# One more block's output by seven half products, its operand sums put on GpSimd and VectorE, and an earlier start of the second stage

## The chip, the cores and the metric

The kernel runs on one core of a Trainium2 chip. The metric is the time of one execution on the device in microseconds (us). A kernel is run several times in turn with the kernel before on the same chip. Each kernel is judged by the runs of the kernel before that were made beside it on its chip.

The engines are named as the profile names them: PE is TensorE (matmuls), PEld its weight loads, DVE is VectorE, ACT is ScalarE, POOL is GpSimd. SBUF and PSUM are two memories of the core: the kernel's operands lie in SBUF, TensorE's products go to PSUM, and a bank is a part of PSUM. A tag such as L386 is a line of the kernel. The lines of the changed kernel mostly lie one further down than those of the kernel before (L385 there is L386 here).

## The reference

```python
scores = (q_c @ k_c.T) / 8          # batch 8, heads 8, seq 576, dim 64, chunks of 64
attn = softmax(scores)              # inside each chunk of 64
x = (attn @ v_c)                    # laid out as 4608 tokens x 512
a = x @ w_a                         # 512 -> 1536
b = x @ w_b
out = (a * b) @ w_out               # 1536 -> 512, float32
```

## The kernel before

The attention works on units of 256 tokens (18 units), the feed-forward part on blocks of 512 tokens (9 blocks). TensorE is the engine that everything else is meant to keep busy.

- Block 0 computes its two projections plainly, in 12 steps of 512 columns (`ab_step`, ft 0 to 11). The attention of unit 2 is woven into its last steps.
- Block 1 computes them in 24 half steps of 256 columns, since unit 3 comes later than unit 2. It starts when `xT` of unit 2 is there.
- Blocks 2 to 8 use six groups each of seven half-size products in place of eight (a Strassen-like scheme). The price is sums of the operands, made beforehand: `combine_x` makes s1 to s4 of the tokens, `combine_w` makes t1 to t4 of the weights.
- The output of a block is made during the next block, in pieces between the products. Blocks 2 and on use seven half products for that too (`OutGroup`, 14 pieces). Their sums are `combine_ab` (of a\*b, tiles `so` and `ab_sb`) and `combine_wo` (of w_out, tiles `wot` and `wo`). The outputs of blocks 0 and 1 are plain.

The parts that the change and the argument touch, with cuts marked:

```python
def cast(U, names="qkv"):                       # float32 -> bfloat16
    for n in names if U < NU else "":
        raw[n, U] = raw_pool.tile([128, 2, H, D], BF16, name=f"{n}_raw")
        eng = nc.vector if U == 0 and n != "v" else nc.gpsimd
        eng.tensor_copy(out=raw[n, U], in_=staged.pop((n, U)))

def transpose_pe(U, names="qk"):
    # ...
        tp = bank().bitcast(BF16).rearrange("c (i m p) -> c i m p", i=2, m=NKT)   # ONE PSUM bank
        for i in range(2):
            # ... four transposes into tp[:, i] ...
        for i in range(2):
            cp = nc.vector.tensor_copy if w == 0 or U == 1 else nc.scalar.copy
            cp(out=dst[:, i], in_=tp[:, i].rearrange("c m (g p) -> c m g p", g=2))

def combine_wo(part, j):                         # sums of w_out, 128x512 f16, both operands in SBUF
    # ...
    o, x0, x1, op = (
        (t3, b22, b12, SUB), (t2, t3, b11, ADD), (t4, b21, t2, SUB), (t1, b12, b11, SUB)
    )[part]                                      # t1 lies in the place of b12
    nc.gpsimd.tensor_tensor(out=o, in0=x0, in1=x1, op=op)

def combine_ab(K, part, j, eng=None):            # sums of a*b, 128x512 f16, both operands in SBUF
    # ...
    o, x0, x1, op = (
        (s1, a21, a22, ADD), (s2, s1, a11, SUB), (a21, a11, a21, SUB), (s4, a12, s2, SUB)
    )[part]
    (eng or nc.gpsimd).tensor_tensor(out=o, in0=x0, in1=x1, op=op)

class Group:                                     # seven products of one group; each is 4 matmuls
    # p1, p6, p2, p5, p7, p3, p4; ScalarE copies results to u_sb, v_sb, b_sb
    def add7(self):                              # VectorE; p4 adds into pc after it
        self.c = c_pool.tile([128, 512], FP32, name="c_sb")
        nc.vector.tensor_tensor(out=self.c, in0=self.C, in1=self.v, op=ADD)
        nc.vector.tensor_tensor(out=self.C, in0=self.C, in1=self.u, op=ADD)
```

```python
# block 0, with the attention of unit 2
for ft in range(NFT):
    ab_step(0, ft)
    # ...
    if ft == 6:
        transpose_pe(2)
    if ft == 8:
        slot(2)                 # scores
    if ft == 10:
        slot(None, 2)           # sums, inverse (Ln and Exp on ScalarE), values -> xT of unit 2

# blocks 2 to 8; the order here is each engine's order of issue
for K in range(2, NBLK):
    for i in range(NWP):
        if i == 1:
            # K == 2: the plain output pieces of block 1 become available here
            # K > 2:  combine_ab(K - 1, 3, j) for j in 0..2, on GpSimd
        # ... bring(unit): loads and casts of the next unit; combine_wo pieces in block 2 ...
        now = Group(K, i)
        now.p1()
        if last:
            last.add7()
        chunk(...)              # output pieces
        if last:
            last.p3()
        # ...
        now.p6()
        if last:
            last.p4()
            finish(last)
        now.p2()
        chunk(...)
        now.p5()
        now.p7()
        last = now
```

The softmax here doesn't subtract the row's maximum and nothing guards it: scores larger than these inputs give would overflow.

## Time and profile before

The kernel before takes 310.87 us (median of 3 runs, 310.45 to 311.45). Its profiled execution has a span of 309.1 us.

| | before |
|---|---|
| TensorE busy | 293.2 of 309.1 us (95%) |
| mean granted TensorE clock | 1.00 |
| first matmul of the projections | 18.87 us |
| first half product of block 1 | 43.43 us, after a gap of 1.47 us |
| groups 0 and 1 of block 2 together | 9.14 us |

Below is the first table of the page of the kernel before: the busy time, its share of the span and the number of instructions for each engine.

```profile
PE 293.2 (95%) x3476; PEld 228.9 (74%) x3478; DVE 205.2 (66%) x342; ACT 194.0 (63%) x350; POOL 178.6 (58%) x168
```

This is the timeline of VectorE before: start, duration, engine, line, operation, output and inputs, shape, count, and in brackets the idle time before it with what ended it.

```profile
80.95 0.43 DVE L385 TENSOR_TENSOR s<-xT 128x512 f16<-128x512 f16 x1
...
82.09 1.26 DVE L385 TENSOR_TENSOR s<-xT,s 128x512 f16<-128x512 f16 x1
83.27 0.41 DVE L364 SCALAR_TENSOR_TENSOR ab_sb<-po,c_sb 128x256 f16<-128x256 f32 x1
83.60 2.33 DVE L129 TENSOR_TENSOR wa<-wa,wb 128x512 f16<-128x512 f16 x2
87.67 0.69 DVE L443 TENSOR_TENSOR c_sb<-pc,v_sb 128x512 f32<-128x512 f32 x1 [1.74 <-ACT v_sb L416]
```

The first and the second line are the same operation of the same shape: 0.43 us and 1.26 us. GpSimd is idle from 80.40 to 81.81, while the first runs; a cast of its own from 81.81 to 83.07 lies beside the second. The two sums `wa<-wa,wb` (2.33 us for both) run beside it too. The last line is `add7` of the first group.

The gap in front of block 1 shows in the timelines of TensorE and ScalarE. The first line is the first half product of block 1. The second is the Exp of unit 2's `inverse`, on which its `xT` depends.

```profile
43.43 0.60 PE L355 MATMUL pa<-xT,wb 128*128 128x256 f16 x4 [1.47 <-DVE xT L305]
...
41.00 1.06 ACT L282 ACTIVATE ln<-ln 128x1024 f32<-128x1024 f32 x1
```

### The profile page before, as it was taken

To read this page: it belongs to the slowest core of one execution; us is meant where nothing else is said; L and a number is where in the kernel's file an instruction comes from. 1 tells how busy PE (TensorE), PEld (TensorE's weight loads), DVE (VectorE), ACT (ScalarE), POOL (GpSimd) and SP (SyncE) were. 2 spreads that over 40 slices of the span, in tenths; PEclk is the share of its full clock that TensorE was granted. 3 is DMA by queue.
4 is the path that set the end of the run, shared out by engine and by line. 5 is a ranking of instruction groups with operands and counts; after the bars stand their busy time and mean duration, and the time that the engine had idled before them with its cause. 6 is when DMAs were issued, how large, how long until landed. Compare 5 with 4: busy or idle time off the path is not lost.

```text
span 309.1 us, 8485 instructions
## 1 busy us (share of the span) xinstructions
PE 293.2 (95%) x3476; PEld 228.9 (74%) x3478; DVE 205.2 (66%) x342; ACT 194.0 (63%) x350; POOL 178.6 (58%) x168
## 2 busy tenths in 40 slices
PE   2879989999999999999999999999999999999995
PEld 1534557866566768888888888888888888888884
DVE  3345663967866686567757776677668766965872
ACT  1643557448575657766877686768775867566531
POOL 0575656644538688936782777377737711780560
PEclk9999999999999999999999999999999999999999
DMA  7999999999989994698439943993493000300025
GB/s 233 303 382 279 274 326 344 246 228 200 272 209 221 222 240 120 91 251 220 125 70 244 241 130 86 215 293 94 102 174 134 6 0 2 136 3 3 0 77 197
DMA packets 138887, 54.03 MB, mean 175 GB/s; under 512 B 114016, under 2 KB 132960, under 8 KB 138848
## 3 DMA queue, kind: packets, MB, share of 16 engines
q1 hardware_dynamic: 138704, 53.36, 70.8%
q8 instruction: 27, 0.44, 0.6%
q10 hardware_dynamic: 144, 0.13, 0.1%
q14 instruction: 12, 0.10, 0.1%
HBM read 37.75 MB, written 9.44 MB: 153 GB/s over the span
## 4 chain that ended last, share of the span: by engine, by line
PE 81%; DVE 6%; ACT 4%; POOL 4%; issue 2%; DMA 2%; SPq 0%; DVEq 0%; POOLq 0%; ACTq 0%
PE pb L405 17%; PE pc L405 11%; PE pa L405 10%; PE po L541 9%; PE pq L541 8%; PE pb L609 3%; PE pb L355 3%; PE pc L355 3%; PE po L355 3%; DMA st<-in_q_dram 2%; PE pq L355 2%; POOL so L485 2%; PE pa L355 2%; PE pt L296 1%; PE pt L263 1%
## 5 line engine op out<-in xcount | busy, mean ns | idle before, releaser
L405 PEld LDWEIGHTS <-t 128*128 128x128 f16 x504 | 48.3, 98 | 9.9 <-issue 3.9
L443 DVE TENSOR_TENSOR c_sb<-pc,v_sb 128x512 f32<-128x512 f32 x42 | 28.8, 686 | 35.7 <-ACT v_sb L416 35.0
L485 POOL TENSOR_TENSOR so<-ab_sb 128x512 f16<-128x512 f16 x20 | 23.1, 1152 | 50.9 <-DVE ab_sb L455 50.9
L405 PE MATMUL pb<-s,wa 128*128 128x256 f16 x336 | 50.6, 273 | 0.1
L405 PE MATMUL pa<-xT,wb 128*128 128x256 f16 x336 | 50.4, 273 | 0.0
L416 ACT COPY u_sb<-pb 128x512 f32<-128x512 f32 x42 | 24.7, 587 | 24.8 <-PE pb L405 23.5
L541 PEld LDWEIGHTS <-ab_sb 128*128 128x128 f16 x336 | 32.9, 98 | 4.2 <-issue 0.4
L405 PEld LDWEIGHTS <-wb 128*128 128x128 f16 x336 | 32.9, 98 | 4.0
L405 PEld LDWEIGHTS <-wa 128*128 128x128 f16 x336 | 31.0, 98 | 6.2 <-issue 0.2
L203 POOL CAST k_raw<-st 128x1024 bf16<-128x1024 f32 x17 | 18.1, 1062 | 28.8 <-DMA st<-in_k_dram 28.8
L455 DVE SCALAR_TENSOR_TENSOR ab_sb<-pc,c_sb 128x512 f16<-128x512 f32 x42 | 28.9, 688 | 6.9 <-PE pc L405 5.5
L455 DVE SCALAR_TENSOR_TENSOR ab_sb<-pb,b_sb 128x512 f16<-128x512 f32 x42 | 28.8, 687 | 2.8 <-PE pb L405 2.4
L416 ACT COPY v_sb<-pb 128x512 f32<-128x512 f32 x42 | 24.9, 592 | 8.1 <-PE pb L405 8.1
L423 ACT COPY pb<-pa 128x512 f32<-128x512 f32 x42 | 24.6, 586 | 8.4 <-PE pa L405 8.3
L416 ACT COPY b_sb<-pa 128x512 f32<-128x512 f32 x42 | 25.0, 595 | 7.7 <-PE pa L405 7.7
L444 DVE TENSOR_TENSOR pc<-pc,u_sb 128x512 f32<-128x512 f32 x42 | 29.0, 689 | 0.0
L203 POOL CAST v_raw<-st 128x1024 bf16<-128x1024 f32 x18 | 19.2, 1065 | 15.6 <-DMA st<-in_v_dram 9.3
L305 DVE TENSOR_TENSOR xT<-pt,ln 128x512 f16<-128x512 f32 x30 | 19.4, 684 | 12.2 <-PE pt L296 12.2
L541 PEld LDWEIGHTS <-so 128*128 128x128 f16 x252 | 24.6, 98 | 3.4 <-issue 0.5
L203 POOL CAST q_raw<-st 128x1024 bf16<-128x1024 f32 x17 | 17.9, 1056 | 13.4 <-DMA st<-in_q_dram 12.8
L405 PE MATMUL pb<-s,t 128*128 128x256 f16 x168 | 25.3, 273 | 0.4 <-ACT pb L423 0.4
L405 PE MATMUL pc<-s,t 128*128 128x256 f16 x168 | 25.2, 272 | 0.5 <-DVE ab_sb L455 0.5
(132 smaller groups left out, 578.9 us busy)
## 6 DMA issues: line engine op xcount, KB each, us to landing
out_dram<-o_sb SPq DMA_DIRECT2D x34, 256.0 KB, 3.4
st<-in_v_dram SPq DMA_DIRECT2D x32, 256.0 KB, 4.2
st<-in_q_dram SPq DMA_DIRECT2D x23, 256.0 KB, 4.8
st<-in_k_dram SPq DMA_DIRECT2D x23, 256.0 KB, 3.5
st<-in_moe_w_b_dram SPq DMA_DIRECT2D x6, 512.0 KB, 8.0
st<-in_moe_w_a_dram SPq DMA_DIRECT2D x6, 512.0 KB, 8.0
st<-in_moe_w_out_dram SPq DMA_DIRECT2D x6, 512.0 KB, 6.7
st<-in_q_dram SPq DMA_DIRECT2D x4, 512.0 KB, 5.6
```

The lines of the kernel that those rows point to most:

```text
L203: eng.tensor_copy(out=raw[n, U], in_=staged.pop((n, U)))
L305: nc.vector.tensor_tensor(out=x.rearrange("p m (g c s) -> p m g c s", g=2, c=2)[:, :, :, cl, :], in0=av[cl], in1=rs[:, cl].rearrange("p m ...
L355: nc.tensor.matmul(ps[n], w_ab[n, i][:, kt, o:o + 128], xT[:, kt, c0:c1], start=(kt == 0), stop=(kt == NKT - 1),)
L405: nc.tensor.matmul(t[:, h * 256:h * 256 + 256], w[:, kt, h * 128:h * 128 + 128], x[:, kt], start=start and h == 0 and kt == 0, stop=h == 1 ...
L416: nc.scalar.copy(out=t, in_=src)
L423: nc.scalar.copy(out=self.B, in_=self.A)
L443: nc.vector.tensor_tensor(out=self.c, in0=self.C, in1=self.v, op=ADD)
L444: nc.vector.tensor_tensor(out=self.C, in0=self.C, in1=self.u, op=ADD)
L455: nc.vector.scalar_tensor_tensor(out=self.dst[:, :, c0:c0 + 256], in0=t.rearrange("p (h n) -> p h n", h=2), scalar=AB_SCALE, in1=o.rearran ...
L485: (eng or nc.gpsimd).tensor_tensor(out=o, in0=x0, in1=x1, op=op)
L541: nc.tensor.matmul(t[:, c0:c0 + 256], a[:, kt, th * 128:th * 128 + 128], w[:, kt], start=n in (0, 4) and first and kt == 0, stop=last and ...
L609: nc.tensor.matmul(out_ps[K, tg], ab_tiles[K][:, ft, tg * 128:tg * 128 + 128], wo_sb[:, ft], start=(ft == 0), stop=(ft == NFT - 1),)
```

## The change

The intent has three parts. Block 1's output is made by the seven half products too: 84 matmuls of 256 columns in place of 48 of 512. Its 9 + 9 sums go to GpSimd during block 1, which looks free there, and the last 6 to VectorE at the start of block 2. In the first unit the copies out of PSUM are shared by VectorE and ScalarE, so that the start is shorter. And unit 2's sums and inverse come one step sooner, so that block 1 need not wait for them. Two things come along with these: one dummy matmul and other banks before the last output piece of block 0, and, since the table of output pieces for block 2 is dropped, the first piece already in group 0 (it was in group 1). The diff, with cuts marked:

```diff
-    def combine_wo(part, j):
+    def combine_wo(part, j, eng=None):
 ...
-        nc.gpsimd.tensor_tensor(out=o, in0=x0, in1=x1, op=op)
+        (eng or nc.gpsimd).tensor_tensor(out=o, in0=x0, in1=x1, op=op)
 ...
-            eng = nc.vector if U == 0 and n != "v" else nc.gpsimd
+            eng = nc.vector if (n, U) in (("q", 0), ("k", 0), ("k", 1)) else nc.gpsimd
 ...
             for i in range(2):
-                cp = nc.vector.tensor_copy if w == 0 or U == 1 else nc.scalar.copy
+                dve = i == 0 if U == 0 or (U, w) == (1, 0) else w == 0 or U == 1
+                cp = nc.vector.tensor_copy if dve else nc.scalar.copy
 ...
+        scores(0)
         transpose_pe(1, "q")
-        scores(0)
 ...
+            if ft == 9:
+                sums(2)
+                inverse(2)
             if ft == 10:
-                slot(None, 2)
+                values(2)
+
+        def combine_wo_all(part, eng=None):
+            for j in range(3):
+                combine_wo(part, j, eng)
 
         cast(4)
         cast(5)
         load(6)
+        combine_wo_all(0)
 ...                                             # in half(ft, u), block 1
+            if u == 1 and ft % 2 and ft > 6:
+                for part in range(3):
+                    combine_ab(1, part, ft // 2 - 3)
 ...
         bring(6)
+        combine_wo_all(1)
 ...
         bring(7)
+        combine_wo_all(2)
         h(1)
-        spread[:] = [psum_a, psum_q]
+        spread[:] = [psum_q, psum_o]
 ...
         h(1)
+        whole = bank(psum_q)
+        nc.tensor.matmul(whole, warm_in[:, :128], warm_in, start=True, stop=True)
         out_0(3)
 ...                                             # chunks[2], chunks[3], wo_sums dropped
                 if i == 1:
                     if K == 2:
-                        outs += [ ... out_part(1, tg, p, ...) for tg in range(4) for p in range(3) ]
-                    else:
-                        for j in range(3):
-                            combine_ab(K - 1, 3, j)
+                        combine_wo_all(3, nc.vector)
+                    for j in range(3):
+                        combine_ab(K - 1, 3, j, nc.vector if K == 2 else None)
 ...
-                if K > 2 and i == 0:
+                if i == 0:
                     g = OutGroup(K - 1)
```

## The prediction

> **What bounds the kernel.** TensorE is busy 293.2 of 309.1 us (95%, first table of the page). It is idle mostly in the first 19 us, and in small gaps after: 1.47 us at 41.9-43.4 (timeline of PE: the first half product of block 1 waits for `xT` of unit 2, which waits for the Ln/Exp pair on ScalarE at 39.9-42.1), 0.3-0.5 us at about 54, 76, 84, 110, 114. GpSimd is 58% busy over the span and until 83 us mostly waits for DMA (waits and timeline of POOL).
>
> **What the change does, costed from the trace.**
> 1. Block 1's output: 48 matmuls of 512 columns (12 pieces of 0.864 us = 10.4 us in the chain) become 84 of 256 columns (14 pieces of 0.655 us = 9.2 us). Saves 1.2 us of PE. Two pieces move into the first group of block 2. One extra dummy matmul waits for a ScalarE copy: costs about 0.3 us.
> 2. First unit: halved copies (0.67 us each) on two engines, scores before the transposes of unit 1, one cast on VectorE: the first matmul of the projections comes about 0.7 us sooner (18.9 to 18.1). But k of unit 2 is cast at 30.3-31.4 when its DMA lands, and its transposes follow at 31.5 already: I expect nearly all of the 0.7 us to be lost there.
> 3. Unit 2's normalizing one step sooner removes the 1.47 us gap; v's cast (ends 39.3) and k of unit 3 (42.5) still allow it. Worth about 1.5-1.8 us with step 2.
> 4. GpSimd: nine weight sums and nine sums of block 1 (1.12-1.15 us each) move before or among the casts of units 6 and 7. By its timeline GpSimd ends unit 5 at 65.4. Then, in its program order: weight sums to 68.8, unit 6 to 73.3, weight sums to 76.7, sums j=0,1 to 83.5, unit 7 to 86.6, weight sums to 90, s1 and s2 of j=2 to 92.3. Sharing with VectorE adds to this: the 128x512 f16 sums of VectorE take 0.41 us alone, up to 1.27 beside a GpSimd instruction, as the Trainium skill ("GPSIMD Engine Reference", Specifications: shared SBUF interfaces) lets expect; so 93-95.
> 5. VectorE gets six sums at the start of group 1 of block 2. The last needs s2 of j=2, and in VectorE's order it stands before the first group's sums into `pc`. So p4 of the first group, which PE would reach at about 89, waits to about 95. I expect a PE stall of 4 to 7 us there. The skill ("TensorE: Matmul & The Clock Gate", Part 1) says an idle window of about 3.4 us halves the clock; that would add about 1 us. Before has no such stall after its start to check it (eight transposes took 1.03 us at the start, 0.61 warm).
> 6. Blocks 2, 3 lose GpSimd's 12 weight sums: small gaps at 110-131, about 0.5 us.
>
> **Sum.** -1.7 (2,3) +0.3 -1.2 (1) -0.5 (6) +5.5 (5) +1 (clock) = about +3: I predict 313.8 us, range 307.5 to 317.0. Faster by over 2%: 0.02; within: 0.87; slower: 0.11.
>
> **What would show it.** Right: GpSimd busy without a gap from 73 to 93; VectorE idle or waiting for GpSimd's `so` before `c_sb` of block 2's first group; a PE gap of 4-7 us near 89-95; output pieces of 0.65 us; no gap at 42; the first projection at 18.1 but the transposes of k of unit 2 still at 31.5. Slower matmuls after the stall would show the clock.
>
> **What would make it wrong.** If GpSimd reaches s2 of j=2 sooner (loads landing sooner, sums shorter), the stall vanishes and about 307.5 is left. If VectorE's sums all collide with GpSimd, block 1 stretches and the time passes 317.

## More of the kernel before

Times of groups are read from the ScalarE copy `pb<-pa` that follows a group's first product: a mark that each group has once.

TensorE is the bottleneck, so a change is worth what it does to TensorE's gaps and to its count of columns. The averages of the others (66%, 63%, 58%) promise room. The next view takes the averages apart. It gives, for two stretches around the boundary of blocks 1 and 2, the stretch and its length, then the busy us (and instructions) of PE, PEld, DVE, ACT and POOL, then the granted clock, the share of DMA and GB/s.

```profile
65.00:83.00 18.00, 17.45 (x244) 10.88 (x242) 12.09 (x25) 11.88 (x23) 7.07 (x7) 1.00 1.07 228
83.00:98.00 15.00, 14.49 (x198) 10.36 (x197) 9.79 (x15) 10.86 (x20) 9.47 (x10) 1.00 1.10 217
```

In these 33 us GpSimd is busy for 16.5. It looks like the place for more sums.

In groups 0 and 1 of block 2, TensorE has one small gap, and it waits for ScalarE there:

```profile
84.25 0.60 PE L405 MATMUL pb<-s,t 128*128 128x256 f16 x4 [0.36 <-ACT pb L423]
```

## The result

| | before | after |
|---|---|---|
| median of the shared rounds | 310.88 us (310.45 to 311.45, 4 runs) | 317.83 us (317.69 to 318.66, 4 runs) |
| span of the profiled execution | 309.1 us | 316.0 us |
| mean granted clock | 1.00 | 0.989 |

The ratio is 1.0228, with a 95% interval of 1.0204 to 1.0252. The changed kernel is slower by 2.3%. A ratio here is the mean time of one kernel's fast runs over that of the other's of the same rounds, so it is not quite the ratio of the medians quoted. The prediction was 313.8 us with a range of 307.5 to 317.0, and it gave "slower by over 2%" a chance of 0.11. It was wrong: the result lies above its range.

Where the time went, by the marks:

| mark | before | after | after minus before |
|---|---|---|---|
| first half product of block 1 | 43.43 | 43.54 | +0.11 |
| block 2, group 0 | 83.61 | 84.43 | +0.82 |
| block 2, group 2 | 92.75 | 102.48 | +9.73 |
| block 3, group 0 | 114.18 | 123.27 | +9.09 |
| block 4, group 0, and constant after it | 146.80 | 153.68 | +6.88 |

Nearly everything happens in groups 0 and 1 of block 2. They took 9.14 us before and 18.05 after. The start gained nothing. Here is the first table of the page after, and the row of the granted clock in 40 slices.

```profile
PE 295.2 (93%) x3513; PEld 233.5 (74%) x3515; DVE 217.3 (69%) x347; ACT 198.4 (63%) x356; POOL 186.3 (59%) x173
...
PEclk9999999999977999999999999999999999999999
```

TensorE's busy time rose, although it was given fewer columns. The two sevens say why: its clock was lowered for two slices. VectorE's average is still only 69%. The windows show what the average hides: the same two stretches, and finer ones behind them, after the change.

```profile
65.00:83.00 18.00, 17.60 (x242) 10.81 (x240) 14.76 (x23) 12.10 (x23) 17.27 (x15) 1.00 1.07 229
83.00:98.00 15.00, 9.58 (x97) 6.59 (x95) 14.96 (x15) 7.34 (x13) 14.92 (x14) 0.89 0.92 201
...
85.00:90.00 5.00, 3.55 (x51) 2.62 (x51) 5.00 (x6) 2.17 (x5) 5.00 (x5) 0.78 0.65 88
...
95.00:100.00 5.00, 2.57 (x18) 1.66 (x21) 3.66 (x5) 1.17 (x2) 5.00 (x5) 0.80 0.92 221
```

From 83 to 98 us VectorE is busy for 14.96 of 15 us, and so is GpSimd (14.92). VectorE has 15 instructions there, as many as before (15), but they take 14.96 us in place of 9.79. TensorE is busy for 9.58. Its two gaps, from its timeline:

```profile
86.45 0.81 PE L542 MATMUL po<-wo,ab_sb 128*128 128x256 f16 x6 [2.11 <-DVE ab_sb L365]
...
97.43 0.60 PE L406 MATMUL pc<-xT,t 128*128 128x256 f16 x4 [3.30 <-DVE pc L445]
```

The first is the first output piece. It waits for block 1's last product `ab_sb`, which stands behind the four sums of `combine_x` in VectorE's queue. The second is p4 of group 0, which waits for `add7`. Both wait for VectorE. This is VectorE's timeline after the change, to be read against the one before:

```profile
81.36 0.93 DVE L386 TENSOR_TENSOR s<-xT 128x512 f16<-128x512 f16 x1
...
84.81 1.25 DVE L386 TENSOR_TENSOR s<-xT,s 128x512 f16<-128x512 f16 x1
85.98 0.41 DVE L365 SCALAR_TENSOR_TENSOR ab_sb<-po,c_sb 128x256 f16<-128x256 f32 x1
86.32 2.09 DVE L129 TENSOR_TENSOR wa<-wa,wb 128x512 f16<-128x512 f16 x2
88.33 3.96 DVE L158 TENSOR_TENSOR wo<-wo 128x512 f16<-128x512 f16 x3
92.21 3.96 DVE L486 TENSOR_TENSOR so<-ab_sb,so 128x512 f16<-128x512 f16 x3
96.09 0.68 DVE L444 TENSOR_TENSOR c_sb<-pc,v_sb 128x512 f32<-128x512 f32 x1
```

There is no bracket on any line: the profile shows no wait of VectorE here. It worked without a pause, and its sums of two SBUF operands took 1.25 to 1.37 us each (3.96 for three), where the same shape takes 0.41 to 0.43 when GpSimd is idle. The operations that read PSUM kept their time (0.68 us against 0.69, 0.41 against 0.41). GpSimd beside it, from its timeline:

```profile
88.10 3.91 POOL L158 TENSOR_TENSOR wot<-wo,wot 128x512 f16<-128x512 f16 x3
91.97 1.33 POOL L486 TENSOR_TENSOR so<-ab_sb 128x512 f16<-128x512 f16 x1
93.38 1.22 POOL L486 TENSOR_TENSOR so<-so,ab_sb 128x512 f16<-128x512 f16 x1
```

GpSimd pays too: three weight sums take 3.91 us, where three take 3.38 with VectorE out of the way (that number is from the experiment `late_on_pool` below). Both engines then advance one instruction every 1.3 us, in turn.

The Trainium skill ("SBUF — State Buffer", Who interferes with whom) says: "A DVE instruction with two SBUF inputs contends with a GpSimd instruction that reads SBUF". It also says that an instruction whose operands are not both in SBUF does not, outside certain modes. This trace agrees on both: 0.41 became up to 1.37 for the former, and 0.69 stayed 0.68 for the latter.

At the start, these lines answer to the two shown of before: TensorE's first half product of block 1, ScalarE's Exp of unit 2 and the copy behind it, and VectorE's product that needs this copy.

```profile
43.54 0.60 PE L356 MATMUL pa<-xT,wb 128*128 128x256 f16 x4 [0.64 <-DVE xT L306]
...
40.04 1.06 ACT L283 ACTIVATE ln<-ln 128x1024 f32<-128x1024 f32 x1
41.00 0.57 ACT L364 COPY v_sb<-pb 128x512 f32<-128x512 f32 x1
...
41.60 0.69 DVE L365 SCALAR_TENSOR_TENSOR ab_sb<-pc,v_sb 128x512 f16<-128x512 f32 x1 [1.85 <-ACT v_sb L364]
```

The Exp is indeed earlier by 0.96 us. But it now stands in ScalarE's queue before the copy `v_sb` of step 10, so that copy comes at 41.00. VectorE must take the product of step 10 before it may turn to `xT` of unit 2, and waits 1.85 us for it. The gap shrank from 1.47 to 0.64 us and did not vanish. (This is read from the trace. `start2` below puts the Exp behind that copy and has no gap here, but it also moves unit 2's transposes.)

### The profile page after: what moved, and what is told of

Its sections match the earlier page's. It is cut to its first block, busy times and chain, and to the rows that moved or that the text cites. A ratio compares the mean times of both kernels' runs of the same rounds, so it can differ in the third digit from the quotient of the medians.

```text
span 316.0 us, 8575 instructions
## 1 busy us (share of the span) xinstructions
PE 295.2 (93%) x3513; PEld 233.5 (74%) x3515; DVE 217.3 (69%) x347; ACT 198.4 (63%) x356; POOL 186.3 (59%) x173
## 4 chain that ended last, share of the span: by engine, by line
PE 79%; DVE 8%; DMA 7%; issue 2%; ACT 2%; POOL 1%; SPq 0%; DVEq 0%; ACTq 0%; POOLq 0%
PE pb L406 18%; PE pc L406 12%; PE pa L406 11%; PE po L542 11%; PE pq L542 9%; DMA st<-in_k_dram 4%; PE pb L610 3%; DMA st<-in_moe_w_b_dram 3%; DVE so L486 2%; PE po L356 2%; PE pt L297 2%; PE pc L356 2%; PE pt L249 2%; PE pt L264 1%; PE pq L356 1%
## 5 line engine op out<-in xcount | busy, mean ns | idle before, releaser
L486 POOL TENSOR_TENSOR so<-ab_sb 128x512 f16<-128x512 f16 x23 | 26.9, 1169 | 54.5 <-DVE ab_sb L456 54.5
L406 PE MATMUL pa<-xT,wb 128*128 128x256 f16 x336 | 51.1, 275 | 0.0
L542 PEld LDWEIGHTS <-ab_sb 128*128 128x128 f16 x384 | 38.2, 99 | 7.6 <-issue 2.7
L203 POOL CAST k_raw<-st 128x1024 bf16<-128x1024 f32 x16 | 16.9, 1054 | 27.4 <-DMA st<-in_k_dram 27.2
L542 PEld LDWEIGHTS <-so 128*128 128x128 f16 x288 | 28.1, 98 | 3.4
L406 PE MATMUL pc<-xT,t 128*128 128x256 f16 x168 | 25.2, 272 | 3.3 <-DVE pc L445 3.3
L486 POOL TENSOR_TENSOR so<-so,ab_sb 128x512 f16<-128x512 f16 x23 | 26.7, 1160 | 1.8
L486 POOL TENSOR_TENSOR ab_sb<-ab_sb 128x512 f16<-128x512 f16 x23 | 27.1, 1179 | 0.0
```

The costliest lines, as they stand in the source:

```text
L406: nc.tensor.matmul(t[:, h * 256:h * 256 + 256], w[:, kt, h * 128:h * 128 + 128], x[:, kt], start=start and h == 0 and kt == 0, stop=h == 1 ...
L542: nc.tensor.matmul(t[:, c0:c0 + 256], a[:, kt, th * 128:th * 128 + 128], w[:, kt], start=n in (0, 4) and first and kt == 0, stop=last and ...
```

## The experiments

Twelve runs were made, of eleven kernels (`late2` was run twice). Two theories for the loss in block 2 stood against each other:

- Theory A: VectorE is slow, because its sums of two SBUF operands take turns with an unbroken row of GpSimd instructions. What VectorE has to do before `add7` of group 0 is too long.
- Theory B, the prediction's: VectorE waits. Its last sum needs s2, GpSimd is late with s2, and `add7` stands behind that sum.

A third cause was looked at beside them: the lowered clock.

### Which part loses: the start alone, the output alone

`start_only` is the kernel before with the first unit's changes and unit 2's earlier normalizing; `out_only` is the changed kernel with these two undone.

```diff
 # start_only, against before
-            eng = nc.vector if U == 0 and n != "v" else nc.gpsimd
+            eng = nc.vector if (n, U) in (("q", 0), ("k", 0), ("k", 1)) else nc.gpsimd
-                cp = nc.vector.tensor_copy if w == 0 or U == 1 else nc.scalar.copy
+                dve = i == 0 if U == 0 or (U, w) == (1, 0) else w == 0 or U == 1
+                cp = nc.vector.tensor_copy if dve else nc.scalar.copy
+        scores(0)
         transpose_pe(1, "q")
-        scores(0)
+            if ft == 9:
+                sums(2)
+                inverse(2)
             if ft == 10:
-                slot(None, 2)
+                values(2)
 # out_only, against after: the same edits in reverse
```

> The kernel before with only the first unit's changes and unit 2's earlier normalizing. Theory (each split copy pair runs one after the other, since the trace of the change shows the ScalarE copy starting only when VectorE's ends, and k of unit 2 lands late): no gain, first projection near 19.0 us, block 1 starts near 43.5 us, time within 0.3 us of before (310.9). Rival (these parts gain their 1.7 us and the rest of the change loses more): 309.2 us.

> The kernel before with only block 1's output by seven products and its sums. Theory (all of the loss is here): 317.5 us to 318, PE gaps of about 2 and 3 us at 84 and 94. Rival (start and output interact, shifting GpSimd): clearly below 316.

`start_only` took 311.13 us (309.71 to 312.22, 4 runs), ratio 0.9998, interval 0.9949 to 1.0047: no gain to be seen. `out_only` took 319.21 us (318.70 to 320.45, 4 runs), ratio 1.0264, interval 1.0229 to 1.0299, somewhat slower than the 317.5 to 318 us that were expected. The whole loss is in the output's part. Its two groups took 19.12 us (85.69 to 104.81).

### Off VectorE, on GpSimd: the six late sums

```diff
-                        combine_wo_all(3, nc.vector)
+                        combine_wo_all(3)
                     for j in range(3):
-                        combine_ab(K - 1, 3, j, nc.vector if K == 2 else None)
+                        combine_ab(K - 1, 3, j)
```

> The change with the six sums of block 2's second group put on GpSimd again. Theory A (PE waits at 94 because VectorE's queue is filled with sums that alternate with GpSimd's): the second gap goes, the sums into pc come near 90, 3 to 5 us gained, 313 to 315. Theory B (PE waits for GpSimd's late results, whoever adds them): the wait only moves to the output pieces that need them, under 1 us gained, about 317.

It took 313.13 us (312.01 to 314.38, 4 runs), ratio 1.0064, interval 1.0023 to 1.0105. The two groups took 11.78 us (85.07 to 96.85) in place of 18.05. TensorE's gaps around them, and `add7` on VectorE:

```profile
86.70 0.81 PE L542 MATMUL po<-wo,ab_sb 128*128 128x256 f16 x6 [1.72 <-DVE ab_sb L365]
93.34 0.60 PE L406 MATMUL pc<-xT,t 128*128 128x256 f16 x4 [0.24 <-DVE pc L445]
...
91.99 0.69 DVE L444 TENSOR_TENSOR c_sb<-pc,v_sb 128x512 f32<-128x512 f32 x1 [3.21 <-ACT v_sb L417]
```

With the six sums off VectorE the gap of 3.30 us before p4 is 0.24, and VectorE has 3.21 us to spare. The first gap is still there (1.72 against 2.11): there the piece waits behind the sums of `combine_x` before 86 us, which this edit does not touch. So there are two places where VectorE is late. This run alone does not decide between A and B: the sum that needs s2 went away with the others.

### The dependency on s2 taken away

Here the sum that needed s2 reads a11 in its place, so VectorE needs nothing from GpSimd there. The result is wrong on purpose (relative error 0.298).

```diff
-            (s1, a21, a22, ADD), (s2, s1, a11, SUB), (a21, a11, a21, SUB), (s4, a12, s2, SUB)
+            ... (s4, a12, a11 if K == 1 else s2, SUB)
```

> The change with the three last sums of VectorE's burst reading two halves of block 1's product instead of GpSimd's results (wrong result on purpose; same sizes, no wait for GpSimd's sums). Theory A (VectorE is late because each of its f16 sums takes turns with a GpSimd instruction): those sums still take about 1.3 us each, the sums into pc still come near 96, time within 1 us of the change's 317.8. Theory B (VectorE is late because it waits for GpSimd's last result): the sums into pc come by 93 or sooner and over 2 us are gained.

It took 318.39 us (317.79 to 318.79, 4 runs), ratio 1.0231, interval 1.0199 to 1.0263: no different from the change itself (1.0228). Its VectorE timeline:

```profile
88.76 3.96 DVE L158 TENSOR_TENSOR wo<-wo 128x512 f16<-128x512 f16 x3
92.64 3.96 DVE L486 TENSOR_TENSOR so<-ab_sb 128x512 f16<-128x512 f16 x3
96.52 0.68 DVE L444 TENSOR_TENSOR c_sb<-pc,v_sb 128x512 f32<-128x512 f32 x1
```

Without the dependency the three `so` sums take 3.96 us as before. Theory B falls.

### The row on GpSimd shortened

The nine sums of a\*b on GpSimd were cut to 8 of their 256 columns. Their instructions, order and dependencies stay; only their length goes. The result is wrong on purpose (relative error 0.459).

```diff
+        cut = (lambda t: t[:, :, 0:8]) if K == 1 and part < 3 else (lambda t: t)
-        (eng or nc.gpsimd).tensor_tensor(out=o, in0=x0, in1=x1, op=op)
+        (eng or nc.gpsimd).tensor_tensor(out=cut(o), in0=cut(x0), in1=cut(x1), op=op)
 # and the two so tiles are set to zero at the start, so that nothing reads unwritten memory
```

> The change with GpSimd's nine sums of block 1 cut to 8 of 256 columns (wrong result on purpose), same order, same waits. Theory A and B both say that the second gap goes; A also says that VectorE's sums before it fall from about 1.25 us to about 0.41 us wherever GpSimd now stands still, so the first gap (2.1 us at 84) goes too: block 2's first two groups take under 10.5 us instead of 18.1, time 309 to 312. If the first gap stays near 2 us, something else than GpSimd makes VectorE late there.

It took 311.01 us (310.54 to 311.74, 4 runs), ratio 0.9997, interval 0.9966 to 1.0028: the loss is gone. VectorE's timeline:

```profile
86.77 1.96 DVE L158 TENSOR_TENSOR wo<-wo 128x512 f16<-128x512 f16 x3
88.65 1.08 DVE L487 TENSOR_TENSOR so<-ab_sb,so 128x512 f16<-128x512 f16 x3
90.87 0.69 DVE L444 TENSOR_TENSOR c_sb<-pc,v_sb 128x512 f32<-128x512 f32 x1 [1.14 <-ACT v_sb L417]
```

VectorE's own instructions are unedited. With GpSimd out of the way the three `so` sums take 1.08 us in place of 3.96, and VectorE waits for ScalarE again, as in the kernel before. That is Theory A, shown for the second gap. A part was missed: the two groups took 11.70 us (84.04 to 95.74) where less than 10.5 was expected, and the first gap, which was expected to go, stayed:

```profile
85.58 0.81 PE L543 MATMUL po<-wo,ab_sb 128*128 128x256 f16 x6 [1.63 <-DVE ab_sb L365]
```

The cast of unit 7's v (81.29 to 82.33) and three weight sums that were not shortened (82.30 to 86.21) now lay beside the `combine_x` sums, three of which took 1.17 to 1.37 us, so VectorE was still late for the first output piece. For the first gap this run therefore decides nothing.

### The clock

Dummy matmuls were put into the two gaps, so that TensorE never stood still for long.

```diff
                 now.p1()
+                if (K, i) == (2, 0):
+                    keep_warm(8)
 ...
                 now.p6()
+                if (K, i) == (2, 1):
+                    keep_warm(12)
                 if last:
                     last.p4()
```

> The change with 8 dummy matmuls before the first output piece of block 2's first group and 12 ahead of the late p4, where PE stood still. If the lowered clock after the two gaps costs about 3 us, it goes to 314.5 to 316 with the clock at 1.0 throughout; if the clock costs nothing that matters, 317.8 or more.

It took 316.78 us (315.62 to 317.86, 4 runs), ratio 1.0180, interval 1.0140 to 1.0219. The windows of this run at the place of the low ones above, and the gap before p4 that was left:

```profile
85.00:90.00 5.00, 4.64 (x69) 3.28 (x67) 5.00 (x6) 2.92 (x7) 5.00 (x5) 1.00 0.58 131
...
95.00:100.00 5.00, 3.18 (x57) 2.67 (x57) 4.04 (x7) 2.31 (x4) 4.41 (x5) 1.00 1.25 176
...
96.82 0.60 PE L406 MATMUL pc<-xT,t 128*128 128x256 f16 x4 [1.99 <-DVE pc L445]
```

The granted clock stayed at 1.00, where it had been 0.78 and 0.80. VectorE is as full as before (5.00 of 5.00). The two groups took 16.49 us (83.85 to 100.34) in place of 18.05: the clock cost 1.56 us. It is a follower of the gaps, not their cause. The profiled run was the fastest of the four, and the clock of the slowest was 0.995. Over all runs the ratios differ by 0.0048, about 1.5 us, though their intervals overlap a little. The time expected if the clock mattered (314.5 to 316) was missed: it cost about half of the 3 us supposed there.

This run also gives the size of VectorE's delay without the clock in it. Dummies of 0.216 us each filled part of the gaps: 8 × 0.216 + 0.36 left over, and 12 × 0.216 + 1.99. Together that is 6.67 us. In the change itself only 2.11 + 3.30 = 5.41 us show as gaps, because the slowed matmuls used up the rest.

### The same work at other times

If A holds, the loss should go when VectorE's six sums are taken away and nothing urgent stands behind the others. `late` has all 24 sums on GpSimd. Six weight sums, and behind the casts of unit 7 the s1 and s2 of a\*b, are issued before block 2, the others in block 2. The first output piece comes one slot later.

```diff
 # late, against after
-            if u == 1 and ft % 2 and ft > 6:
-                for part in range(3):
-                    combine_ab(1, part, ft // 2 - 3)
         bring(7)
-        combine_wo_all(2)
+        for j in range(2):
+            for part in range(2):
+                combine_ab(1, part, j)
 ...
+        for part in range(2):
+            combine_ab(1, part, 2)
+            2: (0, 1, 1, 1, 1, 1, 2, 2, 1, 1, 1, 2),         # output pieces of block 2 by slot
                 if i == 1:
-                    if K == 2:
-                        combine_wo_all(3, nc.vector)
                     for j in range(3):
-                        combine_ab(K - 1, 3, j, nc.vector if K == 2 else None)
+                        combine_ab(K - 1, 2 if K == 2 else 3, j)
+                if K == 2 and i == 0:
+                    combine_wo_all(3)
+                if K == 2 and i == 3:
+                    for j in range(3):
+                        combine_ab(1, 3, j)
+                    combine_wo_all(2)
```

> A version meant to keep the 1.2 us: all 24 sums on GpSimd, unit 7's casts ahead of them, only the sums that the first pieces need during block 1, the others in block 2 where GpSimd was idle 100 to 116 us, output pieces from the second slot on. Theory: no gap over 0.5 us in block 2's first groups, 308.5 to 310.5. If GpSimd's later sums miss their pieces, PE gaps of 1 to 3 us in front of the output pieces, 311 to 313.

It took 310.92 us (310.62 to 312.02, 4 runs), ratio 1.0004, interval 0.9966 to 1.0043. The loss is gone, and the expected small gain is not there: a miss. Its window from 83 to 98 us, and VectorE's last `combine_x` sum with the product that the first output piece needs:

```profile
83.00:98.00 15.00, 14.58 (x212) 11.67 (x211) 11.43 (x15) 11.63 (x22) 14.77 (x14) 1.00 0.92 199
...
84.07 1.37 DVE L386 TENSOR_TENSOR s<-xT,s 128x512 f16<-128x512 f16 x1
85.37 0.41 DVE L365 SCALAR_TENSOR_TENSOR ab_sb<-po,c_sb 128x256 f16<-128x256 f32 x1
```

GpSimd is as busy as in the changed kernel (14.77 of 15 us against 14.92), and TensorE has no loss (14.58 of 15). Yet VectorE's sums are slow beside it here too: three of the `combine_x` sums took 1.29 to 1.37 us, and `ab_sb` began at 85.37, as late as in `pool_short` (85.11), where TensorE stood for 1.63 us. What differs is what TensorE needs at that time. The first output piece comes a slot later, and `add7`, with no six sums before it, has 0.61 us to spare. So the first gap has two parts: VectorE's slow sums, and the change's own placing of a piece in the first slot. No run moved that piece alone. The GpSimd row harms when VectorE has sums of two SBUF operands to do beside it, just ahead of something that TensorE waits for. What remained in `late` was a gap of 0.68 us at 99.65, an output piece that waits for ScalarE's copy `uo_sb`.

### Why the shared copies gained little: one bank or two

At the start, the change gives the two halves of one PSUM bank to two engines. The first line is ScalarE's pair of copies before; the other three are the first two copies on VectorE and ScalarE after, and ScalarE's next.

```profile
7.98 1.33 ACT L225 COPY qkt<-pb 128x512 bf16<-128x512 bf16 x2 [5.97 <-PE pb L217]
```

```profile
6.80 0.73 DVE L226 COPY qkt<-pt 128x512 bf16<-128x512 bf16 x1
...
7.56 0.73 ACT L226 COPY qkt<-pt 128x512 bf16<-128x512 bf16 x1 [5.55 <-DVE qkt L226]
8.78 0.73 ACT L226 COPY qkt<-pb 128x512 bf16<-128x512 bf16 x1 [0.48 <-DVE qkt L226]
```

The copy on ScalarE begins when that on VectorE ends (6.80 + 0.73). The two do not overlap: the pair takes 0.73 + 0.73 us on two engines, where one engine took 1.33. The bracket names VectorE's copy as what ScalarE's copy waited for, although neither reads what the other writes. The Trainium skill ("PSUM — Partial Sum Buffer", PSUM bank collisions raise a hardware error) gives the reason for such an order: two engines may not access one bank, in the same quadrant, at the same time, and reads against reads are included. To test it, `two_banks` puts the halves of unit 0 into two banks.

```diff
-            tp = bank().bitcast(BF16).rearrange("c (i m p) -> c i m p", i=2, m=NKT)
+            tps = [
+                bank().bitcast(BF16).rearrange("c (i m p) -> c i m p", i=2, m=NKT)
+                for _ in range(2 if U == 0 else 1)
+            ]
 ...
-                        tp[:, i, m, :],
+                        tps[i % len(tps)][:, i, m, :],
 ...
-                cp(out=dst[:, i], in_=tp[:, i].rearrange("c m (g p) -> c m g p", g=2))
+                cp(out=dst[:, i], in_=tps[i % len(tps)][:, i].rearrange("c m (g p) -> c m g p", g=2))
```

> The change with the first unit's transposes in two PSUM banks per tensor, one for each copying engine, so that the ScalarE copy waits for PE and not for VectorE's copy. Theory: the two copies overlap, scores of unit 0 come about 0.7 us sooner (8.9 instead of 9.6 us) and the first projection 0.5 to 1 us sooner than 19.0, but block 1 still starts 11.3 us after the transposes of k of unit 2, which wait for their DMA; total within 0.7 us of the change. Rival (copies were not what held the start): first projection still at 19.

It took 317.59 us (316.99 to 319.46, 4 runs), ratio 1.0217, interval 1.0175 to 1.0259, with the loss in block 2 still in it. ScalarE's copies of this run:

```profile
6.54 0.73 ACT L229 COPY qkt<-pb 128x512 bf16<-128x512 bf16 x1 [4.52 <-PE pb L220]
...
8.02 0.73 ACT L229 COPY qkt<-pc 128x512 bf16<-128x512 bf16 x1 [0.75 <-PE pc L220]
```

Both now wait for TensorE and run beside VectorE's (6.80 to 7.52). The first projection came at 18.51 us, against 19.04 in the change and 18.87 before. (One run of each says little: `out_only`, whose start is that of before, came at 19.31. But the seven profiled runs with halves in one bank lie at 19.04 to 19.32, and the five with two banks at 17.86 to 18.52.) And yet block 1 started at 43.41. Unit 2's k was the reason: its transposes began at 32.10 us, after 0.90 us of waiting for the cast of its load, which depends on when the load arrives. In all the kernels that have the unit 2 change of this diff and its order of steps (eight profiled runs), block 1 begins 11.29 to 11.31 us after that start of the transposes, whatever came before; in the two without it (before and `out_only`), 11.95 and 11.96. That is the worth of the earlier normalizing: 0.65 us.

### A better start, and a version that beats both

`start2` is `start_only` with two banks for units 0 and 1, the transposes of unit 2 one step later (so that TensorE does not wait for k), and `inverse(2)` behind the copy of step 10 in ScalarE's queue.

```diff
 # start2, against start_only
-            tp = bank().bitcast(BF16).rearrange("c (i m p) -> c i m p", i=2, m=NKT)
+            tps = [
+                bank().bitcast(BF16).rearrange("c (i m p) -> c i m p", i=2, m=NKT)
+                for _ in range(2 if U <= 1 else 1)
+            ]
 ...                                           # transposes and copies use tps as in two_banks
-                dve = i == 0 if U == 0 or (U, w) == (1, 0) else w == 0 or U == 1
+                dve = i == 0 if U <= 1 else w == 0
-            if ft == 6:
+            if ft == 7:
                 transpose_pe(2)
 ...
             if ft == 9:
                 sums(2)
-                inverse(2)
             if ft == 10:
+                inverse(2)
                 values(2)
```

> The kernel before with a start that follows the findings: unit 0's and 1's transposes in one PSUM bank per copying engine, unit 2's transposes one projection step later (so that a late k of unit 2 is not waited for), its inverse behind the ScalarE copy of step 10. Theory (the start gains only if both waits are gone): first projection at 18 us, no PE wait at the transposes of unit 2, block 1 starting near 42 us instead of 43.4, 309.5 to 310.3. Rival (the DMA paces the whole of block 0, so any gain waits for the next load): block 1 still near 43.4, time equal to before.

It took 310.84 us (310.06 to 311.65, 6 runs) beside 311.62 of the kernel before on that chip (11 runs): ratio 0.9972, interval 0.9941 to 1.0003. That is inconclusive by itself, and above the 309.5 to 310.3 expected. Its trace shows the first projection at 18.17 us and block 1 at 42.28, 1.15 us sooner than before. In this run the lead was lost again in block 3: the mark of its group 1 is at 119.44 us, against 119.41 before, after gaps of 0.59 and 0.67 us in which TensorE waited for VectorE. By the trace, VectorE had sums of 0.81 to 1.37 us beside GpSimd ahead of those products, so the same sharing can eat a gain made earlier.

`late2` is `late` with that start, and with the output pieces of block 2 in the order (0, 0, 1, 1, 1, 1, 2, 2, 2, 2, 1, 1).

> The late version with that start, and with the output pieces paired so that a double slot holds both halves of one product (the late version stood 0.68 us before a piece that followed its predecessor's copy). Theory: the gap before the pieces goes and the start's 1.4 us add: 308.5 to 309.5, a ratio near 0.994. If the gap only moves, 310 or more.

It took 309.89 us (309.58 to 311.85, 6 runs), ratio 0.9962, interval 0.9929 to 0.9995, a little above the 308.5 to 309.5 us expected. Four of the six runs were near 309.7 and two near 311.8. The profiled one was of the latter. It shows a new gap: below, one VectorE sum, two GpSimd casts beside it, and TensorE's product that waits at the end.

```profile
109.98 2.48 DVE L389 TENSOR_TENSOR s<-xT 128x512 f16<-128x512 f16 x1
...
109.05 1.04 POOL L203 CAST k_raw<-st 128x1024 bf16<-128x1024 f32 x1
110.03 1.04 POOL L203 CAST v_raw<-st 128x1024 bf16<-128x1024 f32 x1
...
114.41 1.01 PE L409 MATMUL pc<-s,t 128*128 128x256 f16 x4 [2.19 <-DVE ab_sb L459]
```

This sum took 2.48 us, not 1.3. It lasted through the rest of the cast of k, the whole cast of v and the GpSimd sum behind it (111.03 to 112.18): it seems to have been passed over twice. `late3` moves the first three weight sums between the casts of unit 5, to bring GpSimd's row forward by that much; `late2_again` is `late2` once more beside it.

```diff
 # late3, against late2
         cast(4)
-        cast(5)
+        for j, n in enumerate("qkv"):
+            combine_wo(0, j)
+            cast(5, n)
         load(6)
-        combine_wo_all(0)
```

> The second late version with the first three weight sums between the casts of unit 5, where GpSimd stood idle for its loads, so that GpSimd's queue is about 3 us shorter in block 2. Theory (what is left to lose comes from VectorE's f16 sums of block 3's first combination meeting an unbroken row of GpSimd instructions at 110 us, one of which took 2.48 us): that sum falls under 1.4 us, PE waits there under 1 us, ratio to before 0.992 to 0.996. If the sums of block 1 now collide instead (VectorE is busy over 95% at 55 to 63 us), 0.997 or more.

> The second late version once more, beside the third on the same chip: ratio to before 0.994 to 0.998 as in its first run.

`late3` took 309.35 us (308.63 to 312.65, 8 runs), ratio 0.9934, interval 0.9916 to 0.9952; `late2_again` took 309.19 us (308.45 to 310.38, 6 runs), ratio 0.9934, interval 0.9913 to 0.9954. In `late3` the sum took 2.81 us, where less than 1.4 was expected, and TensorE waited 2.52 us, where less than 1 was: the edit missed its aim. In the profiled run of `late2_again` the same sum took 0.76 us; GpSimd's casts had begun 2.2 us sooner there (105.89 against 108.06 in `late2`) and were over. So the same kernel comes out differently at this place from run to run. Which of the engines gets the turn was not settled.

Both versions are faster than the kernel before by about half a per cent (0.7% on one chip, 0.4% on the other) with a correct result; that is below the 2% that counts as faster here. By the ratios to it they are faster than the change by 2.6 to 2.9%.

## Why the prediction was wrong

The ledger, in us. The measured terms come from the marks and runs above; the last but one, the later gaps, is what the marks leave over after the output pieces.

| step of the prediction | predicted | measured |
|---|---|---|
| (2), (3): the start and unit 2's normalizing | −1.7 | +0.1 |
| (1): the dummy matmul, and the rest up to block 2 | +0.3 | +0.7 |
| (1): output in pieces of 0.655 | −1.2 | −1.2 |
| (5): the stall in group 0 and 1 | +5.5 | +6.3 |
| (5): the clock | +1.0 | +1.6 |
| (6): later gaps | −0.5 | −0.8 |
| sum | +3.4, written as +3 | +6.7, of 6.88 by the marks |

- **Output pieces: right.** In the first two groups four pieces of 0.655 stand where two of 0.864 stood (+0.89); after them, ten pieces are each shorter by 0.21 (−2.09). Together −1.2.
- **The stall: the mechanism of this step failed, though its place was right.** Step 5 said that the last sum "needs s2 of j=2" and that p4 waits for it to about 95. The stall is there (p4 at 97.43). But `s4_nodep` took the dependency away and changed nothing. `pool_short` left it in place, made GpSimd's sums short, and the gap before p4 fell to 0.24 us. VectorE did not wait; its sums took 1.3 us each in turn with GpSimd's. VectorE's delay was 6.67 us, and before had a gap of its own of 0.36 in these groups, which leaves 6.3. The prediction knew the 1.27 us and charged it to GpSimd's schedule in step 4, not to VectorE's own row: `combine_x`, `combine_w` and the six new sums, one behind the other, each tripled. Hence it had one gap, where there were two (2.11 and 3.30). That 5.5 and 6.3 lie close is in part luck: without the clock's effect the gap before p4 was 4.58 us, and the first gap, which the prediction did not have, made up the rest. Its sign, "VectorE idle or waiting for GpSimd's `so`", did not appear.
- **GpSimd busy without a gap from 73 to 93: right in the main**, by the windows (17.27 of 18 us and 14.92 of 15), and for longer than that.
- **The clock: right, and somewhat too small.** It cost 1.56 us (`after_warm`). The Trainium skill ("TensorE: Matmul & The Clock Gate", Part 1) speaks of an idle window of about 3.4 us. Here gaps of 2.11 and 3.30 us, with broken work around them, were enough for stretches of 5 us at 0.78 and 0.80.
- **The start: wrong, and the largest error.** This is the step that failed by most, as the prediction put it: "Unit 2's normalizing one step sooner removes the 1.47 us gap ... Worth about 1.5-1.8 us with step 2." It left 0.64 us of the gap and was worth 0.65. The reason, as the trace shows it, is the order of ScalarE's queue: `inverse` moved in front of the copy of step 10, VectorE's product of step 10 moved back behind it, and `xT` stands behind that product. Step 2's other part, "the first matmul of the projections comes about 0.7 us sooner", was wrong too: it came at 19.04, no sooner than with the old start (18.87 before, 19.31 in `out_only`). The halves on two engines did not overlap, since they shared a bank. Only the caution there held: what the start would have gained is lost at k of unit 2, whose transposes wait for their load. They began at 31.5 to 33.0 us over the profiled runs. In the profiled run of the change they began at 32.24, 0.76 later than in that of before, and this ate the 0.65.

The sum missed by 4.0 us (2.9 predicted, 6.9 found). The start makes 1.8 of it, the stall 0.8, the clock 0.6, the step before block 2 0.4. The rounding of the sum from 3.4 to 2.9 adds 0.5, the later gaps take off 0.3, and 0.2 is unexplained. Had only the start been right, the result would have been about 316.0, inside the range. The range was too narrow for the one risk that it named itself: "If VectorE's sums all collide with GpSimd, block 1 stretches and the time passes 317."

Of the +0.7 us between block 1's start and block 2, TensorE's timelines place 0.39 at the dummy matmul (0.42 us behind before just ahead of it, 0.81 just after it), close to the 0.3 predicted, and the other 0.30 between 74.5 and 76.8 us. What caused the latter stays open, and no run tried the dummy alone.

## What to carry to other kernels

Before moving sums to an engine that looks idle, look up which other engine has sums with both operands in SBUF at that time, and price those at their shared duration (1.3 us here, not 0.41). A busy GpSimd cost little when nothing that TensorE soon needed stood behind such sums (`late`); a row as full cost 6.7 us when VectorE had a string of such sums in front of the operations that TensorE waited for. To shorten a copy by splitting it over two engines, give each its own PSUM bank, and when an operation is moved forward in an engine's queue, follow the one that it now stands in front of.

## What the Trainium skill lacked or had wrong

- "SBUF — State Buffer", SBUF: two separate sides: it says that whichever of the two instructions starts first holds the shared ports for the whole instruction, but not who is served next. In most places the engines took strict turns (1.25 to 1.37 us for each VectorE sum), but one sum took 2.48 us in `late2` and 2.81 in `late3`, through more than one GpSimd instruction, and the same sum 0.76 us in another run.
- The same section: if both held these ports for their whole time, a turn of the two would last about as long as both durations, 0.41 + 1.15 = 1.56 us (1.15 is the mean of GpSimd's `so` sums before). Three turns took 3.96 us, or 1.32 each. So the two overlap by a little, or a recorded duration holds some time in which the ports are free; the runs do not tell which.
- "TensorE: Matmul & The Clock Gate", Part 1: it names an idle window of about 3.4 us. Gaps of 2.11 and 3.30 us already went with a mean granted clock of 0.78 and 0.80 over 5 us, and with 1.56 us lost. The page tells of short idles that lowered the clock in another kernel, but gives no way to price them. Length alone does not settle it: a gap of 2.19 us in `late2` went with 0.79 over 110 to 118 us, a gap of 2.52 us in `late3` with 1.00 there.
- "PSUM — Partial Sum Buffer", PSUM bank collisions raise a hardware error: it agrees, and says that the compiler orders two engines that touch the same bank and quadrant. It gives no duration for a copy split over two engines. Here a half on each of two engines took 0.73 + 0.73 us one after the other, against 1.33 for both on one engine.
- No page that was looked up for this tells how much the arrival of one load varies between runs: the transposes of unit 2's k, which wait for TensorE or for the cast of their load, began between 31.5 and 33.0 us in the profiled runs.
